# A fused linear-attention and two-layer MoE kernel: whole-tile output stores, two copying engines and two store queues in the last block, and an earlier last input product

## The chip, the cores and the metric

The kernel runs on one core of one Trainium2 chip, as one launch. The core has a matrix engine (PE, with a separate row PEld for its weight loads), a vector engine (DVE), a scalar engine (ACT), a general engine (POOL) and a sequencer that issues most DMAs (SP); ACT's sequencer can issue DMAs too. The metric is the device time of one execution in microseconds (us). Three runs of the kernel before took 1208.06, 1213.6 and 1229.15 us; the median is 1213.6 us. The profile is of one further execution.

## The reference

The inputs are six arrays of shape 4 x 8 x 768 x 40 (batch, heads, steps, head size) and five weight matrices. A recurrence over 768 steps with a 40 x 40 state for each of the 32 heads gives 3072 rows of 320 numbers. Two feed-forward layers follow, all in fp32.

```python
for t in range(S):
    y[:, :, t] = np.einsum('bhd,bhde->bhe', rt, state)
    Sa = np.einsum('bhde,bhe->bhd', state, at)
    state_decay = state * wt[:, :, None, :] - np.einsum('bhd,bhe->bhde', Sa, bt)
    state = state_decay + np.einsum('bhd,bhe->bhde', vt, kt)
x = y.transpose(0, 2, 1, 3).reshape(B * S, H * D)       # 3072 x 320
h = np.maximum(x @ w_in, 0.0); x = h * h @ w_out         # first layer, 2048 wide
g = x @ w_gate; silu = g / (1.0 + np.exp(-g))
out = silu * (x @ w_val) @ w_out2                        # second layer, 1536 wide
```

## The kernel before

The recurrence is done in chunks of 32 steps, and the first layer runs beside it, block by block. The second layer starts when the recurrence is over, and it is the last third of the program. It works on six blocks (`NB2`) of 512 rows each, as four tiles of 128 rows; of each tile, 64 rows come from one batch and 64 rows from another, because the recurrence handles two batches at a time. For each block it goes through 12 slices (`nf`) of 128 columns of the inner width, so there are 72 pairs `P` of block and slice, and the last pair is 71.

One pair (`pair2`) does this. Eight matmuls make the gate product in the PSUM bank `pg` and eight make the value product in `pv` (tag F2, line 460; every fp32 product is split in a high and a low part, hence three matmuls for one product, and a packed third for the rest of the 320 columns). ACT takes the sigmoid of `pg` (line 1461), DVE multiplies it by `pg` and then by `pv` (line 1464, twice), ACT rounds the result to its high part `gh` (line 436), and DVE makes the low part `gl` (line 1130). Then twelve matmuls, three for each of the four tiles, add the slice to four accumulators in PSUM (tag O, line 1472). After the last slice of a block ACT copies each accumulator to an SBUF tile `o2` (line 436), and SP stores it to the output (line 1481): since the 128 rows of a tile belong at two places of the output, as two DMAs of 64 rows. The view of the output is

```python
outv = out.rearrange("(r t m p) d -> m t r p d", r=nb // 2, t=2, p=64)
```

so that `outv[m, t]` has the shape 2 x 64 x 320, with the two halves 1536 rows apart.

The order on each engine is made by a planner written in the kernel (`Plan`). Each step is told to it by `op(cost, fn, reads, writes, due=..., tag=...)`: `cost` gives the engines that may run it, with a time in us that only the planner uses; a step with two engines is given to the one that would end it first. An engine takes, of the steps that are ready, the one with the smallest `due`. For pair `P` the input products have the due time `NS + DELAY + P` and the output products that plus 0.5. A DMA issue is a step of the engine whose queue it uses. `queues` maps SP and ACT to their DMA queues.

After the last pair comes a test of whether the fast recurrence stayed in range. DVE reduces the recorded maxima to `ok` (lines 1598 to 1604), PE adds them up (`cnt`, line 1606), DVE writes `flag` (line 1607), and every engine loads it and branches over a slow version of the whole computation (lines 1608 and 1609). SP then waits for every DMA that is still out before the program ends (lines 1609 and 1673).

Two other kinds of transfer matter further down. Line 1125 stores the first layer's result, 128 rows of 1280 bytes that stand one behind the other. Line 1382 (`w2_tile`) loads the second layer's weights into the tiles `ws`: for each group, first the gate matrix and then the value matrix, three loads each. The first two loads take 128 rows. The third takes the last 64 rows twice, by a source view of 2 x 64 rows into a tile of 128 partitions:

```python
return w[r0:r0 + 64, c][None].to_broadcast([2, 64, c.stop - c.start]) if last else w[r0:r0 + 128, c]
```

Of the kernel before, what the change touches and what calls it, by code (L numbers as in the profile page):

```python
# [21 lines left out]
DM = H * D  # L22
F1 = 2048
F2 = 1536
# [14 lines left out]
PE, ACT, DVE, POOL, SP = "PE", "ACT", "DVE", "POOL", "SP"  # L39
# [32 lines left out]
class Plan:  # L72
# [31 lines left out]
    def op(self, cost, fn, r=(), w=(), due=0.0, dma=0.0, take=None, give=None, cols=0, tag="", mode=None, act=0, port=False, lag=0.0):  # L104
        o = Op()
        o.cost, o.fn, o.due, o.seq, o.take, o.give, o.cols, o.tag = cost, fn, due, self.n, take, give, cols, tag
        self.n += 1
        o.dma, o.claim, o.mode, o.act, o.port, o.lag = dma, None, mode, act or cols, port, lag
        o.leaves = mode
        o.bulk = bool(cost) and SP in cost and not r  # L110
        o.succ, o.done, o.eng, o.mate = [], None, None, None
        o.ready = {e: 0.0 for e in (cost or self.free)}
        pre = set()
        for k in r:
            if k in self.writer:
                pre.add(self.writer[k])
        for k in w:
            if k in self.writer:
                pre.add(self.writer[k])
            pre.update(self.readers.get(k, ()))  # L120
        o.need = 0
        for p in pre:
            if p.done is None:
                p.succ.append(o)
                o.need += 1
            else:
                self.arrive(o, p)
        for k in r:
            self.readers.setdefault(k, []).append(o)
        for k in w:  # L130
            self.writer[k] = o
            self.readers[k] = []
        if o.need == 0:
            self.offer(o)
        return o
# [237 lines left out]
def tile_kernel(ctx: ExitStack, tc: tile.TileContext, a: dict, out: bass.AP, nb: int, seq: int):  # L373
    nc = tc.nc
# [60 lines left out]
    def copy(e, dst, src):  # L435
        nc.scalar.copy(dst, src) if e == ACT else eng[e].tensor_copy(dst, src)  # L436
# [15 lines left out]
    def in_products(ps, f, xh, xl, hi, lo, hl):  # L452
        c = slice(f * 128, (f + 1) * 128)
        seq_ = (
            (hi[0], xh[:, 0]), (hi[0], xl[:, 0]), (lo[0], xh[:, 0]),
            (hi[1], xh[:, 1]), (hi[1], xl[:, 1]), (lo[1], xh[:, 1]),
            (hl, xh[:, 2]), (hl, xl[:, 2]),
        )
        for i, (w, x) in enumerate(seq_):
            nc.tensor.matmul(ps, w[:, c], x, start=(i == 0), stop=(i == len(seq_) - 1))  # L460
# [154 lines left out]
    op = plan.op  # L615
# [101 lines left out]
    queues = {SP: nc.sync, ACT: nc.scalar}  # L717
# [410 lines left out]
    def split_pair(n, due):  # L1128
        op({ACT: t_act(512)}, lambda e: copy(e, gh[n], two["gr"][n]), (("gr", n),), (("gh", n),), due=due, tag="gh")
        op({POOL: t_pool(512), DVE: t_dve(512)}, lambda e: eng[e].tensor_sub(gl[n], two["gr"][n], gh[n].bitcast(F32)),  # L1130
           (("gr", n), ("gh", n)), (("gl", n),), due=due, tag="gl", port=True)
# [218 lines left out]
    two = {}  # L1350
# [42 lines left out]
    for g in range(NP2):  # L1393
        f = slice(g * 256, (g + 1) * 256)
        due = NS + g
# [11 lines left out]
    outv = out.rearrange("(r t m p) d -> m t r p d", r=nb // 2, t=2, p=64)  # L1407

    NB2 = NBLK // 2
    nf = F2 // 128  # L1410
    assert NBLK % 2 == 0
    acc_keys = [("p", 0), ("p", 1), ("acc", 0), ("acc", 1)]
    ACC2 = [PS[:, 4 + t] for t in range(4)]
# [29 lines left out]
    def pair2(P):  # L1443
        B, f = divmod(P, nf)
        n, b = P % NGR, P % 2
        due = NS + DELAY + P
        ks = [(x, B % 2, t) for x in ("xh2", "xl2") for t in range(4)] + ["WO"] + wkeys[("wi", 2, f // 2)]

        def f_in(kind):
            w = two["w"]  # L1450
            in_products(two["p" + kind][b], f, two["xh"][B % 2], two["xl"][B % 2],
                        *((w.hg, w.lg, w.hlg) if kind == "g" else (w.hv, w.lv, w.hlv)))

        for kind in "gv":
            op({PE: 1.814}, lambda e, kind=kind: f_in(kind), ks, (("p" + kind, b),), due=due, cols=4096, tag="F2")
        kw = dict(due=due)

        def both(x):
            return x[n].rearrange("p h t -> p (h t)")

        op({ACT: 0.478}, lambda e: nc.scalar.activation(both(two["gr"]), two["pg"][b], AF.Sigmoid), (("pg", b),), (("gr", n),),  # L1461
           tag="sig", **kw)
        for q in ("pg", "pv"):
            op({DVE: 0.602}, lambda e, q=q: nc.vector.tensor_mul(both(two["gr"]), two[q][b], both(two["gr"])), ((q, b),),  # L1464
               (("gr", n),), tag="u" + q, **kw)
        split_pair(n, due)
        wk = wkeys[("wo", 2, f // 2)]
        for t in range(4):
            def o_mm(e, t=t):
                c, w = slice(t % 2 * 128, t % 2 * 128 + 128), two["w"]  # L1470
                for i, (x, y) in enumerate(((gh, w.oh), (gh, w.ol), (gl, w.oh))):
                    nc.tensor.matmul(ACC2[t][:, :DM], x[n][:, t // 2, c], y[:, f, :], start=(f == 0 and i == 0),  # L1472
                                     stop=(f == nf - 1 and i == 2))

            op({PE: 0.44}, o_mm, [("gh", n), ("gl", n)] + wk, (acc_keys[t],), due=due + 0.5, cols=960, tag="O")
            if f == nf - 1:
                op({ACT: 0.318}, lambda e, t=t: copy(e, two["o"][t], ACC2[t][:, :DM]), (acc_keys[t],), (("o2", t),),
                   due=due, tag="o")
                d = outv[2 * B + t // 2, t % 2]
                for r in range(2):  # L1480
                    op({SP: 0.42}, lambda e, t=t, d=d, r=r: nc.sync.dma_start(d[r], two["o"][t][64 * r:64 * r + 64]),
                       (("o2", t),), (), due=due, dma=0.455, tag="dma")

    x2_load(0, NS + DELAY)
    for t in range(4):
# [1 line left out]
    for P in range(NB2 * nf):  # L1487
        B, f = divmod(P, nf)
        if B == 0:
            w2_tile(w2_d[W2[2]][f * 128:(f + 1) * 128, :], wkeys[("w2d", W2[2])] + ["WO"], DM,  # L1490
                    lambda f=f: (two["w"].oh[:, f, :], two["w"].ol[:, f, :]), ("wo", 2, f // 2), NS + DELAY + f)
        pair2(P)
        if B + 1 < NB2:
            if f == 2:
                x2_load(B + 1, NS + DELAY + P)
            if nf - 6 <= f < nf - 2:
                x2_turn(B + 1, f - (nf - 6), "pv", P % 2, NS + DELAY + P + 0.6)
# [188 lines left out]
```

## Time and profile before

| what | value |
|---|---|
| median of three runs | 1213.6 us (1208.06 to 1229.15) |
| the profiled execution | 1212.33 us |
| span of the profile, from its first to its last instruction | 1210.3 us |
| mean granted PE clock | 0.968 |
| PE busy | 1113.8 us, 92% of the span |
| DVE, ACT busy | 639.5 us (53%), 551.8 us (46%) |

The profiled execution is 2 us longer than its span. All times in the rows below are counted from the start of the span, so the program ends at 1210.3. A "q" behind an engine's name means its sequencer, which waits, branches and issues DMAs. In the table of stretches the columns are the length, the busy time of each engine, the granted PE clock (1.00 is full speed), the share of the 16 DMA engines' time that was busy, and GB/s.

### The profile page before, as it was taken

What the parts mean: (1) busy time and instruction counts of PE and PEld (TensorE: products, weight loads), DVE (VectorE), ACT (ScalarE), POOL (GpSimd) and SP (SyncE); (2) the same over time, 40 slices, a digit from 0 to 9 for tenths busy, and PEclk for the clock granted to TensorE, in tenths of its full rate; (3) what the DMA queues carried; (4) which work ended last, traced back from release to release, by engine and by line L of the source; (5) the groups of instructions that cost most, each with busy time, mean ns of one, the idle gap of its engine ahead of it and who ended that gap; (6) DMA issues with size and microseconds to landing.
All of it is one profiled execution on the core that took longest, in us unless ns stands there. A gap on an engine that the chain in (4) does not pass through costs nothing.

```text
span 1210.3 us, 42859 instructions
## 1 busy us (share of the span) xinstructions
PE 1113.8 (92%) x18640; PEld 1011.7 (84%) x18640; DVE 639.5 (53%) x1496; ACT 551.8 (46%) x1275; POOL 97.1 (8%) x122
## 2 busy tenths in 40 slices
PE   7487978989889899999998999899999999999995
PEld 7376877888888798999898899888888888888884
DVE  4766885676657475856473422445334343434432
ACT  6344985555555464645453444654223222222221
POOL 0221331011011011210000000000000000000000
PEclk9788998999999999999999999899999999999998
DMA  5645664565655465544443322422101010100001
GB/s 137 159 112 155 163 172 121 141 179 142 172 134 148 136 175 157 151 130 99 109 102 77 69 58 65 132 86 83 35 7 26 18 27 22 27 23 1 22 1 25
DMA packets 171393, 114.96 MB, mean 95 GB/s; under 512 B 104092, under 2 KB 147644, under 8 KB 171196
## 3 DMA queue, kind: packets, MB, share of 16 engines
q1 hardware_dynamic: 168556, 110.52, 35.1%
q8 instruction: 148, 2.42, 0.9%
q10 hardware_dynamic: 2640, 1.61, 0.5%
q14 instruction: 49, 0.40, 0.1%
HBM read 88.35 MB, written 23.72 MB: 93 GB/s over the span
## 4 chain that ended last, share of the span: by engine, by line
PE 67%; DMA 5%; DVE 5%; issue 3%; SPq 2%; ACT 1%; DVEq 0%; ACTq 0%
PE ps L460 31%; PE ps L465 11%; PE ps L1472 10%; DMA ws<-f_moe_w_val 3%; SPq L723 2%; PE ps L1057 2%; PE ps L1038 2%; PE ps L1029 1%; PE ps L960 1%; PE ps L973 1%; PE ps L1072 1%; PE ps L802 1%; PE ps L999 1%; PE ps L868 1%; PE ps L954 1%
## 5 line engine op out<-in xcount | busy, mean ns | idle before, releaser
L1464 DVE TENSOR_TENSOR gr<-ps,gr 128x512 f32<-128x512 f32 x144 | 99.5, 692 | 168.4 <-PE ps L460 86.4
L1146 ACT ACTIVATE ps<-ps 128x512 f32<-128x512 f32 x192 | 111.6, 581 | 106.9 <-PE ps L460 104.3
L465 PE MATMUL ps<-o1h,gh 128*128 128x320 f32 x384 | 131.9, 343 | 4.0 <-ACT gh L436 3.9
L436 ACT CAST gh<-gr 128x512 fp32r<-128x512 f32 x72 | 44.8, 622 | 177.1 <-DVE gr L1464 177.1
L465 PE MATMUL ps<-o1l,gh 128*128 128x320 f32 x384 | 121.5, 316 | 2.7 <-issue 2.7
L465 PE MATMUL ps<-o1h,gl 128*128 128x320 f32 x384 | 122.5, 319 | 0.3 <-DVE gl L413 0.3
L460 PE MATMUL ps<-xh,w1h 128*128 128x256 f32 x384 | 117.1, 305 | 0.0
L460 PE MATMUL ps<-xl,w1h 128*128 128x256 f32 x384 | 109.9, 286 | 0.0
L460 PE MATMUL ps<-xh,w1l 128*128 128x256 f32 x384 | 109.8, 286 | 0.0
L413 DVE TENSOR_TENSOR gl<-ps,gh 128x512 fp32r<-128x512 f32 x96 | 65.8, 685 | 59.0 <-ACT gh L436 58.9
L1472 PE MATMUL ps<-o2h,gh 128*128 128x320 f32 x288 | 89.0, 309 | 1.9 <-ACT gh L436 1.4
L1472 PE MATMUL ps<-o2l,gh 128*128 128x320 f32 x288 | 88.8, 308 | 0.2 <-DVE o2l L1389 0.2
L1472 PE MATMUL ps<-o2h,gl 128*128 128x320 f32 x288 | 88.7, 308 | 0.2 <-DVE gl L1130 0.2
L465 PEld LDWEIGHTS ps<-o1h,gh 128*128 128x128 f32 x384 | 74.2, 193 | 9.8 <-ACT gh L436 4.7
L1461 ACT ACTIVATE gr<-ps 128x512 f32<-128x512 f32 x72 | 43.2, 599 | 81.2 <-PE ps L460 79.6
L465 PEld LDWEIGHTS ps<-o1h,gl 128*128 128x128 f32 x384 | 74.7, 195 | 4.6 <-issue 2.5
L460 PEld LDWEIGHTS ps<-xh,w1h 128*128 128x128 f32 x384 | 74.2, 193 | 1.9
L465 PEld LDWEIGHTS ps<-o1l,gh 128*128 128x128 f32 x384 | 74.8, 195 | 0.1
L1130 DVE TENSOR_TENSOR gl<-gr,gh 128x512 fp32r<-128x512 f32 x72 | 49.9, 693 | 47.1 <-ACT gh L436 47.0
L460 PEld LDWEIGHTS ps<-xl,w1h 128*128 128x128 f32 x384 | 74.5, 194 | 0.0
L460 PEld LDWEIGHTS ps<-xh,w1l 128*128 128x128 f32 x384 | 74.1, 193 | 0.0
L1282 PE MATMUL ps<-warm 128*128 128x256 f32 x302 | 50.6, 320 | 24.3 <-DVE ct L1213 14.5
(170 smaller groups left out, 2702.8 us busy)
## 6 DMA issues: line engine op xcount, KB each, us to landing
wakb<-in_wakb_dram SPq DMA_DIRECT2D x42, 422.5 KB
RB<-in_vr_e_dram SPq DMA_DIRECT2D x44, 208.0 KB
RH<-in_r_e_dram SPq DMA_DIRECT2D x90, 80.0 KB
cx<-in_moe_w_out_dram SPq DMA_DIRECT2D x21, 320.0 KB
room<-xt_d SPq DMA_DIRECT2D x36, 128.0 KB
cx<-in_moe_w_in_dram SPq DMA_DIRECT2D x15, 256.0 KB
xt_d<-yb SPq DMA_DIRECT2D x24, 160.0 KB
x_d<-room SPq DMA_DIRECT2D x24, 160.0 KB
```

Source lines behind the costliest of these rows:

```text
L413: nc.vector.tensor_sub(dst, full, hi.bitcast(F32))
L436: nc.scalar.copy(dst, src) if e == ACT else eng[e].tensor_copy(dst, src)
L460: nc.tensor.matmul(ps, w[:, c], x, start=(i == 0), stop=(i == len(seq_) - 1))
L465: nc.tensor.matmul(acc[t][:, :DM], g[:, half, ts], w[:, f, :], start=(f == 0 and i == 0), stop=(f == nf - 1 and i == 2),)
L723: o = att(cost, lambda e: queues[e].dma_start(dst(), src()), r, w, due=due, dma=dma, tag="dma")
L1038: nc.tensor.matmul(v[64 * p:64 * p + 64, jh, u], RW[:, 4 * jh + 2 * u + p], RB[:, :, s], start=True, stop=True)
L1130: op({POOL: t_pool(512), DVE: t_dve(512)}, lambda e: eng[e].tensor_sub(gl[n], two["gr"][n], gh[n].bitcast(F32)), (("gr", n), ("gh", n)), ( ...
L1146: op({ACT: 0.478}, lambda e, f=f: nc.scalar.activation(P1[b], P1[b], f), (), (("p", b),), due=due, tag="relu")
L1282: nc.tensor.matmul(PS[:, b, 0:256].rearrange("p (a b) -> p a b", a=2), warm, warm[:, None, :].to_broadcast([128, 2, 128]), start=True, sto ...
L1461: op({ACT: 0.478}, lambda e: nc.scalar.activation(both(two["gr"]), two["pg"][b], AF.Sigmoid), (("pg", b),), (("gr", n),), tag="sig", **kw)
L1464: op({DVE: 0.602}, lambda e, q=q: nc.vector.tensor_mul(both(two["gr"]), two[q][b], both(two["gr"])), ((q, b),), (("gr", n),), tag="u" + q, ...
L1472: nc.tensor.matmul(ACC2[t][:, :DM], x[n][:, t // 2, c], y[:, f, :], start=(f == 0 and i == 0), stop=(f == nf - 1 and i == 2))
```

## The change

Four things are changed, all in the second layer.

- Every output tile is stored by one DMA of 2 x 64 rows in place of two DMAs of 64 rows.
- In the last block (`end`) the tiles 0 and 2 are copied by ACT and the tiles 1 and 3 by DVE.
- In the last block a store may be issued by SP or by ACT, as the planner finds it.
- The input products of pair 71 get a due time that is 0.6 smaller, which is before the output products of pair 70.

```diff
         for kind in "gv":
-            op({PE: 1.814}, lambda e, kind=kind: f_in(kind), ks, (("p" + kind, b),), due=due, cols=4096, tag="F2")
+            op({PE: 1.814}, lambda e, kind=kind: f_in(kind), ks, (("p" + kind, b),),
+               due=due - (0.6 if P == NB2 * nf - 1 else 0.0), cols=4096, tag="F2")
...
             if f == nf - 1:
-                op({ACT: 0.318}, lambda e, t=t: copy(e, two["o"][t], ACC2[t][:, :DM]), (acc_keys[t],), (("o2", t),),
-                   due=due, tag="o")
-                d = outv[2 * B + t // 2, t % 2]
-                for r in range(2):
-                    op({SP: 0.42}, lambda e, t=t, d=d, r=r: nc.sync.dma_start(d[r], two["o"][t][64 * r:64 * r + 64]),
-                       (("o2", t),), (), due=due, dma=0.455, tag="dma")
+                end = B == NB2 - 1
+                op(({ACT: 0.43}, {DVE: 0.45})[t % 2] if end else {ACT: 0.318}, lambda e, t=t: copy(e, two["o"][t], ACC2[t][:, :DM]),
+                   (acc_keys[t],), (("o2", t),), due=due, tag="o")
+                op({SP: 0.6, ACT: 0.6} if end else {SP: 0.6},
+                   lambda e, t=t, d=outv[2 * B + t // 2, t % 2]: queues[e].dma_start(d, two["o"][t]),
+                   (("o2", t),), (), due=due, dma=0.6, tag="dma")
```

Ahead of the last 24 output products the rest of the program has the same instructions in the same order on PE, DVE, ACT and POOL; on SP each earlier block has four stores where it had eight, at the same place between the other DMAs.

On PE, at the start of pair 71's value products; `wghl` ends the gate product of pair 71, `wvh` and `wvl` belong to its value product, and `gh0`, `gl0` are the operands of pair 70's output products. Before:

```order
L460 MATMUL ps_113<-xh21_13030,wghl_13037 128x512
L460 MATMUL ps_113<-xl21_13032,wghl_13037 128x512
L1472 MATMUL ps_113<-o2h_13427,gh0_107 128x320
L1472 MATMUL ps_113<-o2l_13428,gh0_107 128x320
L1472 MATMUL ps_113<-o2h_13427,gl0_109 128x320
L1472 MATMUL ps_113<-o2h_13427,gh0_107 128x320
```

The same place after the change:

```order
L460 MATMUL ps_113<-xh21_13030,wghl_13037 128x512
L460 MATMUL ps_113<-xl21_13032,wghl_13037 128x512
L460 MATMUL ps_113<-xh21_13030,wvh0_13038 128x512
L460 MATMUL ps_113<-xl21_13032,wvh0_13038 128x512
L460 MATMUL ps_113<-xh21_13030,wvl0_13040 128x512
L460 MATMUL ps_113<-xh21_13030,wvh1_13039 128x512
```

The eight value matmuls of pair 71 moved ahead of the twelve output matmuls of pair 70; the twelve of pair 71 still come last.

On SP, the last stores, with what each waits for (a DMAHW semaphore is that of an earlier DMA). Before:

```order
L1481 DMA out_dram<-o_13429 64x320 [waits DMAHW2_49,Activation_49]
L1481 DMA out_dram<-o_13429 64x320 [waits DMAHW3_49]
L1481 DMA out_dram<-o_13430 64x320 [waits DMAHW4_49,Activation_49]
L1481 DMA out_dram<-o_13430 64x320 [waits DMAHW5_49]
L1481 DMA out_dram<-o_13431 64x320 [waits DMAHW6_49,Activation_49]
L1481 DMA out_dram<-o_13431 64x320 [waits DMAHW7_49]
L1481 DMA out_dram<-o_13432 64x320 [waits DMAHW0_49,Activation_49]
L1481 DMA out_dram<-o_13432 64x320 [waits DMAHW1_49]
```

After the change, the last two stores of the block before, the three that SP still has in the last block, and the load of the flag behind them:

```order
L1482 DMA out_dram<-o_13431 2x64x320 [waits DMAHW4_49,Activation_49]
L1482 DMA out_dram<-o_13432 2x64x320 [waits DMAHW5_49,Activation_49]
L1482 DMA out_dram<-o_13429 2x64x320 [waits DMAHW6_49,Activation_49]
L1482 DMA out_dram<-o_13430 2x64x320 [waits DMAHW7_49,DVE_49]
L1482 DMA out_dram<-o_13432 2x64x320 [waits DMAHW1_49,DVE_49]
L1609 TENSOR_LOAD flag [waits DVE_49]
```

Eight issues became three, each with the view 2 x 64 x 320 on the output's side.

On ACT, the end of its program after the change (before, four copies stood here and no DMA):

```order
L436 CAST gh_108<-gr_13028 128x512 [waits DVE_49]
L436 COPY o_13429<-ps 128x320 [waits DMAHW2_49,PE_49]
L436 COPY o_13431<-ps 128x320 [waits DMAHW4_49,PE_49]
L1482 DMA out_dram<-o_13431 2x64x320 [waits Activation_49]
L1609 TENSOR_LOAD flag [waits DVE_49]
L1610 COMPARE_AND_BRANCH
```

Two copies went to DVE, where they stand behind the five short instructions of the range test, and the store of tile 2 came to ACT's queue.

## Rows read from the trace of the kernel before

**Rows 1.** The page's first lines: the span, then busy time by engine.

```profile
span 1210.3 us, 42859 instructions
PE 1113.8 (92%) x18640; PEld 1011.7 (84%) x18640; DVE 639.5 (53%) x1496; ACT 551.8 (46%) x1275; POOL 97.1 (8%) x122
```

**Rows 2.** The chain that ended last, its end: start us, us, what.

```profile
1193.60 1.87 PE ps L460 x8
...
1195.49 0.70 DVE gr L1464
...
1196.87 0.70 DVE gl L1130
...
1197.61 1.75 PE ps L1472 x10
...
1199.38 0.44 ACT o L436
```

**Rows 3.** Instructions in order of time, the last 20 us: start us, us, engine, line.

```profile
1191.68 0.31 PE L1472 MATMUL ps<-o2h,gh 128*128 128x320 f32 x1
1192.58 0.69 DVE L1464 TENSOR_TENSOR gr<-ps,gr 128x512 f32<-128x512 f32 x1 [2.23 <-ACT gr L1461]
1193.44 0.39 PE L460 MATMUL ps<-xh,wvh 128*128 128x512 f32 x1
1198.07 1.74 ACT L436 COPY o<-ps 128x320 f32<-128x320 f32 x4 [1.23 <-PE ps L1472]
1198.52 6.09 SPq L1481 DMA_DIRECT2D out_dram<-o  x8
```

**Rows 4.** Lines 1609 and 1673: instructions, ns min/median/max, first and last start us.

```profile
L1609 PEldq COMPARE_BRANCH  x1: 4095/4095/4095, 1200.9 to 1200.9; - x1
L1609 SPq COMPARE_BRANCH  x1: 50/50/50, 1205.8 to 1205.8; - x1
L1609 SPq EVENT_SEMAPHORE  x8: 17/17/17, 1208.3 to 1208.9; - x8
L1673 SPq EVENT_SEMAPHORE  x10: 17/28/28, 1208.9 to 1210.2; - x10
```

**Rows 5.** Stretches with stores in flight: length, engines' busy, PEclk, DMA share, GB/s.

```profile
673.50:674.00 0.50, 0.50 (x60) 0.50 (x64) 0.43 (x2) 0.49 (x1) 0.00 (x0) 1.00 0.97 341
1003.00:1004.00 1.00, 1.00 (x6) 0.83 (x5) 0.23 (x1) 0.49 (x2) 0.00 (x0) 1.00 0.51 123
1206.00:1207.00 1.00, 0.00 (x0) 0.00 (x0) 0.00 (x0) 0.00 (x0) 0.00 (x0) 0.50 0.03 8
```

**Rows 6.** SP's DMA issues in order of time, in two stretches.

```profile
672.58 0.84 SPq L1125 DMA_DIRECT2D x_d<-room  x2
...
771.02 0.50 SPq L1382 DMA_DIRECT2D ws<-f_moe_w_gate  x1
771.61 1.49 SPq L1382 DMA_DIRECT2D ws<-f_moe_w_val  x3
```

**Rows 7.** The chain that ended last, three of its pieces from 761 us on.

```profile
761.92 1.89 DMA x<-x_d
...
763.88 5.25 DMA ws<-f_moe_w_val
...
772.60 7.62 DMA ws<-f_moe_w_val
```

**Rows 8.** Two stretches behind the issues of 771 to 773 us.

```profile
774.50:775.50 1.00, 1.00 (x10) 1.00 (x9) 0.00 (x0) 0.00 (x0) 0.00 (x0) 1.00 0.15 51
775.50:776.50 1.00, 1.00 (x11) 1.00 (x10) 0.00 (x0) 0.00 (x0) 0.00 (x0) 1.00 0.13 45
```

**Rows 9.** Groups by line: a DVE copy, and store issues (ns min/median/max).

```profile
L436 DVE COPY UQ<-ps 128x320 f32<-128x320 f32 x4 | 2.0, 488 | 2.0 <-PE ps L960 1.0 <-ACT ps L436 1.0
L1481 SPq DMA_DIRECT2D out_dram<-o x48: 466/594/1688, 869.1 to 1204.0; - x48
L1125 SPq DMA_DIRECT2D x_d<-room x24: 332/367/767, 192.6 to 805.2; - x24
```

## The prediction

> **What bounds the kernel now.** I read the page first: PE is busy for 1113.8 of 1210.3 us [rows 1], so over the whole program only less PE work would pay, and the change takes none away. What it can move is the program's end, so I read the chain that ended last from its end backwards, then the last 20 us in order of time, then the sequencers' rows, and last the stretches of DMA traffic.
>
> The reader is to see three things at the end. First, PE stands still between its last input product and its last output products: the value product ends at 1195.47 (1193.60 + 1.87), a DVE product, the ACT cast and a DVE difference follow one after the other, and the output matmuls that need the low part start at 1197.61 [rows 2]. Pair 70's twelve output matmuls, which could have filled that hole, are already over: they ran from 1191.68 to 1193.44 [rows 3]. Second, PE ends at 1199.36 and the last copy at 1199.82 [rows 2], but SP issues eight stores from 1198.52 on and needs 6.09 us for them [rows 3], until 1204.61. It loads the flag and branches only then, at 1205.8, and gets to its first wait for a DMA at 1208.3; eight such waits and the closing ones take the rest, 2.0 us, to 1210.3 [rows 4]. Third, DMA traffic is as good as over in 1206 to 1207 (share 0.03) [rows 5], so those waits cost nothing: SP comes late, and the data have landed before it asks. **The end is set by SP's issues, with 5.7 us behind them (1210.3 - 1204.61).**
>
> **The change, part by part.**
>
> *The earlier input product.* Twelve matmuls of pair 70 (1193.44 - 1191.68 = 1.76 us [rows 3]) move behind pair 71's value product. That product ends 1.76 us earlier; DVE's second multiply can start at 1193.73, since the first ends at 1193.27 (1192.58 + 0.69) [rows 3]; cast and difference follow, and the low part is there at 1195.85. PE meanwhile does the twelve, until 1195.44, and the two matmuls that need only the high part, until about 1195.7, so 0.1 us of the hole is left. PE's end moves from 1199.36 to 1197.60. Gain: 1.76 us on this path.
>
> *Two engines copy.* ACT's four copies take 1.74 us back to back [rows 3], 0.435 each, and PE finishes an accumulator every 0.44 us (1.75 / 4 [rows 2]): one engine keeps pace. A DVE copy of this size from PSUM takes 0.488 [rows 9]. The last copy is now DVE's, from about 1197.62 to 1198.11; before, it ended at 1199.82. Two engines gain nothing beyond the 1.76 and lose some 0.05. The five range-test instructions that stand ahead of the DVE copies run in the wait for PE and cost nothing; without that cover they would cost under 1 us.
>
> *Fewer issues, two queues.* SP has three issues in place of eight. A 64-row store took 0.594 us to issue (median), a 128-row one 0.367 [rows 9]; the 2 x 64 load took 0.50 [rows 6]. I take 0.50. The first copy ends at about 1196.75 (1198.07 - 1.76 + 0.435), so the first issue starts at 1196.8, the third follows the last copy at 1198.15, and SP is free at 1198.65, 5.96 us earlier than 1204.61. ACT's one issue starts about 1197.65 and is over before the flag is written. If SP's issues were still what sets the end, the program would end at 1204.3.
>
> *The shape of the stores.* This is the term on which the sign hangs. The new store has 2 x 64 rows on the DRAM side and 128 partitions on the SBUF side. No store of the trace has that shape, but the third load of each weight trio has it, mirrored. Two of these were issued close together, the gate's at 771.02 and the value's at 772.60 (the third of the trio from 771.61), and the latter landed at 780.2 (772.60 + 7.62) [rows 6, 7]; the other loads of the trio are 128-row ones. From 774.5 on the DMA share is 0.13 to 0.15 at 45 to 51 GB/s [rows 8], and 45 GB/s is what carries the two loads' 262,144 bytes from 774.5 to 780.2 (5.8 us). **A share of 0.14 is two engines of sixteen (2/16 = 0.125), and two such transfers together don't reach more: they share the same two.** The value load, queued behind the gate load, took 7.62 us, one with less in its way 5.25, a plain 128-row transfer 1.89 [rows 7]. Two contiguous 128-row stores, issued from 672.58 on [rows 6], ran at 341 GB/s with a share of 0.97 [rows 5], which is 22 GB/s for each engine, so two engines would give 44 GB/s for stores as well.
>
> I take 45 GB/s. One tile is 128 x 1280 = 163,840 bytes and takes 3.64 us; the four take 14.6 us. They are issued within 2 us of each other, so they queue. The fixed part of such a transfer, start and landing, is 5.25 less 131,072 bytes at 45 GB/s (2.9), or 2.3 us. The last store lands at 1196.8 + 2.3 + 14.6 = 1213.7. SP has branched long before (1198.65 plus the 3.7 us that it took from 1204.61 to 1208.3 is 1202.4) and waits. Behind that wait are 1.4 to 2.0 us of the closing, depending on which of the eight semaphores is the late one [rows 4]; I take 1.7. **The program ends at 1215.4, 5.1 us later than now.** The 6 us that PE and SP gain are swallowed by the wait for the landing.
>
> Here the Trainium skill speaks against the change: DMA: Bandwidth & Descriptors, Why a DMA increments its semaphore by 16 and not by 1, says that a DMA runs on the largest number of engines, up to 16, that divides the outermost size of both sides. By that rule a 2 x 64 store gets 2 engines and the old 64-row store 16; the trace's loads agree (share 0.14), and no run here shows it for a store. The sum by the rule is the one above.
>
> *The earlier blocks.* Five blocks store the same way in mid-program. There 14.6 us of queued stores meet nothing: a tile of `o2` is needed again a block later, and PE has no wait on a store. The first and the last output store are 869.1 and 1204.0 [rows 9], five blocks apart, so a block lasts about 67 us. I cost it at nothing; if the cover failed, each would show up as an idle PE at a block's start.
>
> **The bounds.** Slowest: if the two engines move stores only as fast as they went in the 64-row stores, 123 GB/s at a share of 0.51 [rows 5], that is 15 GB/s each, the four take 21.7 us, and the end is at 1222.5, 12.2 us later. Fastest, with two engines for each: if ACT's store ran on other engines than SP's, three would queue (10.9 us) and the end be at 1211.7, 1.4 us later. The rate of loads of the same shape and that of contiguous stores agree, so I stay with 45 GB/s.
>
> **The rivals.**
>
> *The stores spread over all sixteen engines* (the other side, faster). For it: the contiguous 128-row store did, at 0.97 [rows 5], and the landing would be hidden as now. Against it: the loads of this very shape don't. Then SP's issues set the end at 1204.3, or 1205.9 if SP's branch takes the 4.1 us that PE's took in place of its own 2.5, because all engines now branch at once [rows 4]. That is 4.4 to 6.0 us less; about 1207.
>
> The Trainium skill has a rule that leads there: DMA: Bandwidth & Descriptors, Rules for kernel authors, advises one 128-partition transfer over two for the disjoint halves. It would make the first part a plain saving of issue time; the trace's 128-row stores fit it, the 2 x 64 loads don't.
>
> *The stores go slower still.* The 12.2 us above: two engines, at the 15 GB/s of the stores before. For it speaks that those stores are of the same tiles to the same output. Against it: they ran all sixteen engines on 64 partitions, which two engines on 128 do not. Its time is 1225.
>
> *The landing is hidden anyway.* It decides from the point at which the last store lands before SP is ready, 1202.4. With the start at 1199.1 (1196.8 + 2.3) that would need 655,360 bytes in 3.3 us, 199 GB/s, over four times what two engines showed, so it is the first rival or nothing.
>
> **How the numbers follow.** The profiled execution took 1212.33 us, 2 us more than its span, and 1.3 less than the median of 1213.6; 5.1 more makes 1217.4 from the one and 1218.7 from the other. I say 1218. Chances: two engines at about 45 GB/s for all four stores 0.66; ACT's store elsewhere 0.08 (1214 to 1215); the slow rate 0.12 (1225); all sixteen engines 0.14 (1207). The range takes in the second and third cases and most of the spread of runs, and leaves out the fourth but for its upper edge: 1208 to 1228. Every case lies within 1.1% of now, and a measurement of this kernel can tell about 2% from no change, so within 2% has 0.95; the 0.02 and 0.03 on the sides are for the spread of the runs, of which one before was 1.3% over the median.
>
> **What would show it.** Right: after 1200 a long stretch with a DMA share near 0.13 and about 45 GB/s; SP's waits at line 1610 ending near 1214 with PE, DVE and ACT idle for over 14 us; the same thin traffic for some 15 us behind each earlier block; PE without its hole before the last output products and ending near 1197.6. Wrong: a share of 0.5 and more behind the last copies and an end near 1205 (all engines), or thin traffic at about 30 GB/s and an end past 1220. The prediction falls if stores choose their engines otherwise than loads do.

## The result and the profile after

| | median us | runs | range |
|---|---|---|---|
| before, in this comparison | 1217.45 | 20 | 1207.3 to 1229.15 |
| after | 1222.62 | 20 | 1213.27 to 1236.0 |

The ratio is 1.0056, with a 95% interval of 1.0032 to 1.008: the changed kernel is slower, by 4 to 10 us, and within 2%. The ratio is of the runs in the usual state, without a few in a slower one; the medians of all runs differ by 5.2 us. Its profiled execution took 1221.75 us with a span of 1219.8 us (before 1212.33 and 1210.3 [rows 1]).

The spans differ by 9.5 us, but not all of that is the change's. The last block but one gives an anchor, the issue of its first store. First the order of time on SP in the profile after, three of the five earlier blocks and the last block:

```profile
873.39 6.03 SPq L1482 DMA_DIRECT2D out_dram<-o  x4
939.83 6.17 SPq L1482 DMA_DIRECT2D out_dram<-o  x4
...
1139.15 6.00 SPq L1482 DMA_DIRECT2D out_dram<-o  x4
...
1200.99 3.19 SPq L1482 DMA_DIRECT2D out_dram<-o  x3
```

The same stores of the kernel before:

```profile
869.13 5.03 SPq L1481 DMA_DIRECT2D out_dram<-o  x8
935.58 6.05 SPq L1481 DMA_DIRECT2D out_dram<-o  x8
...
1134.89 4.94 SPq L1481 DMA_DIRECT2D out_dram<-o  x8
```

The blocks are 66.44 us apart in both (939.83 - 873.39; before 935.58 - 869.13 = 66.45). The changed profile is 4.26 us late already at its first store, ahead of which both programs do the same, and keeps just that. So 4.26 us belong to the run. **From the anchor to the end, which I call the tail, it is 1210.3 - 1134.89 = 75.41 us before and 1219.8 - 1139.15 = 80.65 us after: the change costs 5.2 us.** The prediction had 5.1. The tail is the measure of all experiments below, because runs of one kernel differ by 20 us, and the tail leaves that out. Each kernel has one profile, so one tail; kernels that end alike agree within 0.2 us (before and e9_earlier, and e4_contig and e10_all, which ran on two chips, in the table below).

What the tail consists of shows in the chain that ended last (start, us, what), which answers to [rows 2]:

```profile
1194.25 3.69 PE ps L460 x16
...
1197.96 0.70 DVE gr L1465
...
1199.34 0.70 DVE gl L1130
...
1200.08 1.75 PE ps L1473 x10
...
1201.85 0.50 DVE o L436
```

The sixteen input matmuls now stand together, and PE goes on to 1201.83 with almost no hole. Less 4.26, that is 1197.57, 1.79 us earlier than the 1199.36 of before. PE, DVE and ACT did what the change wants. Then the end of the sequencers' work, line 1610 (the branch and the waits behind it) and line 1674 (ns min/median/max, first and last start), which answers to [rows 4]:

```profile
L1610 PEldq COMPARE_BRANCH  x1: 3455/3455/3455, 1204.6 to 1204.6; - x1
L1610 SPq COMPARE_BRANCH  x1: 50/50/50, 1207.0 to 1207.0; - x1
L1610 SPq EVENT_SEMAPHORE  x8: 17/17/17, 1214.4 to 1218.4; - x8
L1674 SPq EVENT_SEMAPHORE  x10: 17/28/28, 1218.4 to 1219.7; - x10
```

Before, the eight waits came within 0.6 us [rows 4]; now the first is passed at 1214.4 and the last at 1218.4. SP stands there and waits for DMAs. The stretches show which (columns as in [rows 5]):

```profile
1204.00:1205.00 1.00, 0.00 (x0) 0.00 (x0) 0.00 (x0) 0.00 (x0) 0.00 (x0) 1.00 0.13 31
1212.00:1213.00 1.00, 0.00 (x0) 0.00 (x0) 0.00 (x0) 0.00 (x0) 0.00 (x0) 0.50 0.14 52
1217.00:1218.00 1.00, 0.00 (x0) 0.00 (x0) 0.00 (x0) 0.00 (x0) 0.00 (x0) 0.50 0.04 14
1218.00:1219.00 1.00, 0.00 (x0) 0.00 (x0) 0.00 (x0) 0.00 (x0) 0.00 (x0) 0.50 0.00 0
```

No engine computes, and for 15 us two of sixteen DMA engines (0.125) carry the output, first at some 30 and then at some 50 GB/s. The traffic stops just before SP's last wait is passed. By queue (packets, MB, share), from 1207 to 1213:

```profile
q1 hardware_dynamic: 105, 0.13, 6.5%
q10 hardware_dynamic: 104, 0.13, 6.1%
q14 instruction: 5, 0.04, 2.0%
```

q1 is SP's queue and q10 ACT's: with SP alone (e7_sponly) q10 moves nothing behind the last copies. The two together have 12.6%, so SP's and ACT's stores run on the same two engines. Instructions are loaded beside them (q14) and add to the share, which reaches 0.27 in one of the 15 us (1205 to 1206) and 0.15 to 0.18 in four (1207 to 1211).

The trace also records when each increment of a DMA's semaphore came, though not its size. A store of 64 rows gives sixteen; a store of 2 x 64 rows gives three, one just behind its issue and two as it lands. The last store landed at 1217.92, 16.93 us behind the first issue.

### The profile page after: what moved, and what is told of

Read it like the earlier page. It is cut to its first block, busy times and chain, and to the rows that moved or that the text cites. A ratio compares the mean times of both kernels' runs of the same rounds, so it can differ in the third digit from the quotient of the medians.

```text
span 1219.8 us, 42834 instructions
## 1 busy us (share of the span) xinstructions
PE 1122.4 (92%) x18640; PEld 1020.4 (84%) x18640; DVE 641.2 (53%) x1498; ACT 550.8 (45%) x1273; POOL 97.1 (8%) x122
## 4 chain that ended last, share of the span: by engine, by line
PE 68%; DMA 8%; SPq 3%; issue 2%; DVE 2%; ACT 1%; DVEq 0%; ACTq 0%
PE ps L460 31%; PE ps L465 11%; PE ps L1473 10%; SPq L723 3%; DMA ws<-f_moe_w_val 3%; PE ps L1057 2%; PE ps L1038 2%; PE ps L1029 2%; DMA RB<-in_vr_e_dram 2%; PE ps L960 1%; PE ps L1072 1%; PE ps L973 1%; PE ps L802 1%; PE ps L999 1%; PE ps L868 1%
## 5 line engine op out<-in xcount | busy, mean ns | idle before, releaser
L1282 PE MATMUL ps<-warm 128*128 128x256 f32 x302 | 54.8, 340 | 25.8 <-DVE ct L1213 13.6
```

Of the source, the lines that this page charges most:

```text
L1282: nc.tensor.matmul(PS[:, b, 0:256].rearrange("p (a b) -> p a b", a=2), warm, warm[:, None, :].to_broadcast([128, 2, 128]), start=True, sto ...
```

## The experiments

The theory: a store whose view of the output has two places of 64 rows runs on two DMA engines, and the landing of four of these sets the end. Its rivals: ACT's queue or the copies on DVE cost the time; one transfer of 164 KB takes long whatever its shape; the distance between the places is what costs; the earlier blocks' stores cost it.

| kernel | what differs | tail expected | tail measured |
|---|---|---|---|
| before | | | 75.41 |
| after | | | 80.65 |
| e1_early | before + early input product | 73.65 | 1202.6 - 1128.85 = 73.75 |
| e2_shape | before + 2 x 64 stores in the last block, SP alone | 82.4 | 1215.1 - 1133.24 = 81.86 |
| e3_split | after, all stores as two of 64 rows | 70.0 to 71.7 | 1204.9 - 1133.69 = 71.21 |
| e4_contig | after, last block's tiles in one piece each | 69.3 to 71.0 | 1199.9 - 1129.25 = 70.65 |
| e6_four | after, last block's tiles in four pieces each | 73.4 | 1207.7 - 1132.72 = 74.98 |
| e7_sponly | after, SP alone issues | 80.65 | 1218.3 - 1137.88 = 80.42 |
| e8_act | after, ACT alone copies | 80.65 | 1213.4 - 1132.90 = 80.50 |
| e9_earlier | before + 2 x 64 stores in the earlier blocks | 75.4 | 1212.9 - 1137.36 = 75.54 |
| e10_all | as e4_contig, in all blocks | 70.65 | 1236.3 - 1165.47 = 70.83 |

### e1_early: the early input product alone

```diff
-            op({PE: 1.814}, lambda e, kind=kind: f_in(kind), ks, (("p" + kind, b),), due=due, cols=4096, tag="F2")
+            op({PE: 1.814}, lambda e, kind=kind: f_in(kind), ks, (("p" + kind, b),),
+               due=due - (0.6 if P == NB2 * nf - 1 else 0.0), cols=4096, tag="F2")
```

> The kernel before with the early input product alone: stores, copies and queues as before. Measure for all runs: the tail, from the issue of the first store of the last block but one to the end of the span (before 1210.3 - 1134.89 = 75.41 us, changed kernel 1219.8 - 1139.15 = 80.65 us). Theory (the shape of the stores sets the loss, the early product gains what PE no longer idles): PE's hole closes, SP still issues eight stores behind the copies, tail 73.65 us (1.76 less than before). Rival (the moved product gains nothing, because the copies or SP set the end anyway): 75.4. Rival (the moved product is itself the loss): about 80.

The tail is 73.75 us, 1.66 less than before. The early product is worth what was claimed, and the end follows PE, because SP's eight issues follow the copies. One run took 1204.63 us beside a median of 1212.11 for the kernel before (23 runs, 1201.64 to 1221.73), which tells nothing by itself.

### e2_shape: the shape of the last block's stores alone

```diff
+                if B == NB2 - 1:
+                    op({SP: 0.6}, lambda e, t=t, d=d: nc.sync.dma_start(d, two["o"][t]), (("o2", t),), (), due=due, dma=0.6, tag="dma")
-                for r in range(2):
+                for r in range(2) if B < NB2 - 1 else ():
```

> The kernel before with one part of the change alone: in the last block each tile is stored by one transfer of two places of 64 rows, SP issuing all four; copies by ACT, the order of products and the earlier blocks as before. Theory (a store to two places runs on two DMA engines, 3.64 us a tile, and the landing of the fourth sets the end): first issue as before, last landing about 17 us behind it, tail 82.4 us (7.0 more than before). Rival (the loss comes from two queues or from two engines copying): the tail stays at 75.4 or falls with the fewer issues to about 73. Rival (the loss comes from the earlier blocks' stores): 75.4 too.

The store issues in order of time, and two of the stretches behind them:

```profile
1133.24 4.94 SPq L1483 DMA_DIRECT2D out_dram<-o  x8
...
1196.87 6.57 SPq L1481 DMA_DIRECT2D out_dram<-o  x4
```

```profile
1199.00:1200.00 1.00, 0.00 (x0) 0.00 (x0) 0.00 (x0) 0.00 (x0) 0.00 (x0) 1.00 0.13 31
1211.00:1212.00 1.00, 0.00 (x0) 0.00 (x0) 0.00 (x0) 0.00 (x0) 0.00 (x0) 0.50 0.13 49
```

The first store comes 63.63 us behind the anchor, as before (1198.52 - 1134.89), so nothing ahead of it moved. With SP alone and ACT's copies, the shape by itself costs 6.45 us. The landing of the last came 16.7 us behind the first issue. And a row of its own: **four issues took SP 6.57 us, where eight of 64 rows took 6.09 [rows 3].** Fewer issues did not free SP.

### e3_split: two queues, two copying engines, stores of 64 rows

```diff
-                op({SP: 0.6, ACT: 0.6} if end else {SP: 0.6},
-                   lambda e, t=t, d=outv[2 * B + t // 2, t % 2]: queues[e].dma_start(d, two["o"][t]),
-                   (("o2", t),), (), due=due, dma=0.6, tag="dma")
+                for r in range(2):
+                    op({SP: 0.6, ACT: 0.6} if end else {SP: 0.6},
+                       lambda e, t=t, r=r, d=outv[2 * B + t // 2, t % 2]: queues[e].dma_start(d[r], two["o"][t][64 * r:64 * r + 64]),
+                       (("o2", t),), (), due=due, dma=0.3, tag="dma")
```

> The changed kernel with every tile stored as two transfers of 64 rows again, in all blocks; in the last block both queues issue them (four each), two engines copy, and the input product is early. Theory: all sixteen DMA engines carry each transfer, the last landing comes about 2.3 us behind the last issue, and the tail is 70.0 to 71.7 us (3.7 to 5.4 less than before, 9 to 10.6 less than the changed kernel), about 1213 us where the kernel before takes 1217. Rival (ACT's queue or the copies on DVE cost the time): the tail stays near 80.6. Rival (issues never set the end, the closing does): 73.6, as with the early product alone.

```profile
1133.69 4.94 SPq L1483 DMA_DIRECT2D out_dram<-o  x8
...
1195.53 2.50 SPq L1483 DMA_DIRECT2D out_dram<-o  x4
1195.53 1.39 ACTq L1483 DMA_DIRECT2D out_dram<-o  x2
1197.07 1.26 ACTq L1483 DMA_DIRECT2D out_dram<-o  x2
```

The tail is 71.21 us: 9.4 less than after and 4.2 less than before. With the early product alone it was 73.75, so the two queues help once the stores run on all engines: the last issue ends 64.64 us behind the anchor here and 67.73 in e1_early. The second copying engine doesn't help: the last copy ends at 63.78 here, at 63.12 with ACT alone in e1_early. By the clock the gain isn't shown: 1207.95 us median of 12 runs, ratio to before 0.9998 (0.9962 to 1.0034), an interval that just holds the 4.2 / 1212 = 0.35% that the tail gives.

### e4_contig: the same size of store, in one piece

The rows of the last block are dealt to its tiles anew, so that a tile is 128 rows in a row of the output; the loads of these four tiles take two places of 64 rows each.

```diff
+    outw = out.rearrange("(r t n) d -> r t n d", r=nb // 2, t=2)
...
+            end = B == NB2 - 1
+            src = x2v[2 * B:2 * B + 2, t % 2, 64 * (t // 2):64 * (t // 2) + 64] if end else x2v[2 * B + t // 2, t % 2]
...
+        d = outw[t // 2, t % 2, 128 * B:128 * B + 128]
```

> The changed kernel with the rows of the last block dealt to its four tiles in another way: each tile holds 128 rows that lie in one piece in the output (and is loaded from two places instead). Four stores of 128 rows on two queues as in the changed kernel, the same bytes, the same engines. Theory (two places are the cost, not 128 rows in one transfer): the stores run on all sixteen DMA engines, tail 69.3 to 71.0 us. Rival (a transfer of 164 KB takes that long whatever its shape): tail 80.6. Rival (the loads of two places at the block's head now come late): the distance from the anchor to the first store of the last block grows beyond the changed kernel's 61.84 us.

Its stores in order of time, two stretches, and lines 1617 and 1681 (the branch and the last waits):

```profile
1129.25 5.96 SPq L1489 DMA_DIRECT2D out_dram<-o  x4
...
1191.09 1.72 SPq L1489 DMA_DIRECT2D out_dram<-o  x3
...
1191.97 0.39 ACTq L1489 DMA_DIRECT2D out_dram<-o  x1
```

```profile
1192.00:1193.00 1.00, 0.19 (x2) 0.11 (x2) 0.59 (x2) 0.00 (x0) 0.00 (x0) 1.00 0.95 333
1193.00:1194.00 1.00, 0.00 (x0) 0.00 (x0) 0.00 (x0) 0.00 (x0) 0.00 (x0) 1.00 0.85 304
```

```profile
L1617 SPq EVENT_SEMAPHORE  x8: 17/17/17, 1198.0 to 1198.5; - x8
L1617 PEldq COMPARE_BRANCH  x1: 3635/3635/3635, 1193.9 to 1193.9; - x1
L1617 SPq COMPARE_BRANCH  x1: 50/50/50, 1194.2 to 1194.2; - x1
L1681 SPq EVENT_SEMAPHORE  x10: 17/28/28, 1198.6 to 1199.8; - x10
```

The same bytes in as many transfers on the same queues, and a DMA share of 0.95 at 333 GB/s in place of 0.14 at 50. That excludes the size of a transfer, ACT's queue and the DVE copies as causes. The first store comes 61.84 us behind the anchor, as after (1200.99 - 1139.15), so the loads of two places at this block's head cost nothing. The last store landed 3.2 us behind the first issue, at 1194.3. SP had branched at 1194.2, and its first wait is passed only at 1198.0: now it is the branch, some 3.8 us for SP and 3.6 for PE, that sets the end.

By the clock it is 1206.1 us (median of 12) beside 1212.11, ratio 0.996 (0.9928 to 0.9992): **this version is faster than the kernel before**, by as much as its tail says (4.76 / 1212 = 0.39%), which is less than 2%. It was not timed beside the changed kernel; there only the tails speak, 70.65 against 80.65.

### e6_four: four places

```diff
+    outf = out.rearrange("(r m p) d -> m r p d", r=nb, p=64)
...
-                   lambda e, t=t, d=outv[2 * B + t // 2, t % 2]: queues[e].dma_start(d, two["o"][t]),
+                   lambda e, t=t, d=outf[2 * B + t // 2, :, 32 * (t % 2):32 * (t % 2) + 32] if end else outv[2 * B + t // 2, t % 2]: queues[e].dma_start(d, two["o"][t]),
```

> The changed kernel with the last block's rows dealt so that each tile's store goes to four places of 32 rows (and its load comes from four places in two transfers). Theory (as many DMA engines as places): four engines, about twice the rate of the two, the four tiles take about 7.3 us instead of 14.6, tail about 73.4 us. Rival (distant places are the cost, more of them cost more): 80.6 or above. Rival (anything but one piece falls to two engines): 80.6.

```profile
1198.00:1199.00 1.00, 0.00 (x0) 0.00 (x0) 0.00 (x0) 0.00 (x0) 0.00 (x0) 0.54 0.26 97
1200.00:1201.00 1.00, 0.00 (x0) 0.00 (x0) 0.00 (x0) 0.00 (x0) 0.00 (x0) 0.50 0.25 73
1203.00:1204.00 1.00, 0.00 (x0) 0.00 (x0) 0.00 (x0) 0.00 (x0) 0.00 (x0) 0.50 0.25 43
1204.00:1205.00 1.00, 0.00 (x0) 0.00 (x0) 0.00 (x0) 0.00 (x0) 0.00 (x0) 0.50 0.18 35
```

The share is 0.25, four of sixteen, and the semaphore of each store gets five increments (one and four). Four places at half the distance are faster than two, so more places don't cost by themselves. More engines land the stores sooner, but not in proportion: two 16.9 us behind the first issue, four 11.25, sixteen 3.2 (e4_contig). The distance alone was not varied for a store. Against it as the cause speaks that the third weight load of before takes the same 64 rows twice, at no distance, and also ran at a share of 0.13 to 0.15 [rows 8]. The tail of 74.98 us is 1.6 above what twice the rate would give. The last store landed 11.25 us behind the first issue in place of 9.6, since the rate fell to 73 and then 43 GB/s at the same share (in 1203 to 1204 the loading of instructions has 0.05 of it). Why these four engines went slower there was not settled.

The Trainium skill states the pattern (DMA: Bandwidth & Descriptors, Why a DMA increments its semaphore by 16 and not by 1): for DMAs that SP and ACT issue, the issuing sequencer writes those of the 16 increments whose engines take no part at once, and each engine that does adds one when its data has landed. The counts here agree for stores: sixteen for 64 rows and for 128 rows in one piece, one and two for two places, one and four for four.

### e7_sponly and e8_act: one queue, one copying engine

```diff
-                op({SP: 0.6, ACT: 0.6} if end else {SP: 0.6},
+                op({SP: 0.6},
```

> The changed kernel with SP alone issuing the last block's stores. Theory (the two DMA engines are busy from the first store to the last landing, whoever issues): the first store starts as before, tail 80.65 us, within 0.4. Rival (ACT's queue costs the time, its packets alternating with SP's): tail about 75 to 77. Rival (ACT's issue helps): SP's fourth issue behind three others, tail above 81.5.

```diff
-                op(({ACT: 0.43}, {DVE: 0.45})[t % 2] if end else {ACT: 0.318}, lambda e, t=t: copy(e, two["o"][t], ACC2[t][:, :DM]),
+                op({ACT: 0.43} if end else {ACT: 0.318}, lambda e, t=t: copy(e, two["o"][t], ACC2[t][:, :DM]),
```

> The changed kernel with ACT alone copying the last block's four tiles (two queues, early input product and stores of two places as in the changed kernel). Theory (the first tile's copy comes at the same time, the landings hide the rest): tail 80.65 us, within 0.4. Rival (the copies on DVE, behind its range test, cost the time): tail 2 us or more less than 80.65.

The last block's issues with SP alone:

```profile
1199.72 6.68 SPq L1482 DMA_DIRECT2D out_dram<-o  x4
```

The tails are 80.42 and 80.50 us, 0.23 and 0.15 below the changed kernel: with the stores on two DMA engines neither the second queue nor the second copying engine matters. The copies themselves come no sooner with two engines either: the last ends 63.13 us behind the anchor with ACT alone and 63.19 with both. With SP alone the stores land one after the other (5.9, 9.7, 13.5 and 16.7 us behind the first issue); with both queues the second and the third land late together (13.7 and 13.4), and the last at 16.9. The order changes and the end does not.

### e9_earlier: the earlier blocks alone

```diff
+                if B < NB2 - 1:
+                    op({SP: 0.6}, lambda e, t=t, d=d: nc.sync.dma_start(d, two["o"][t]), (("o2", t),), (), due=due, dma=0.6, tag="dma")
-                for r in range(2):
+                for r in range(2) if B == NB2 - 1 else ():
```

> The kernel before with the change's stores in the earlier blocks alone: one transfer of two places per tile in all blocks but the last, the last block as before (eight transfers of 64 rows, ACT copies, no early product). Theory (the earlier blocks' landings are hidden): blocks still 66.44 us apart by their first stores, tail 75.4 us, within 0.3. Rival (their slow landings, or SP's longer issues, hold back later loads or the last block's first store): blocks further apart than 66.44, or a tail above 76.

The tail is 75.54 us, and the blocks' first stores are 66.44 us apart (938.04 - 871.60). The earlier blocks' stores cost nothing.

### e10_all: one piece in every block

```diff
-            src = x2v[2 * B + t // 2, t % 2]
+            src = x2v[2 * B:2 * B + 2, t % 2, 64 * (t // 2):64 * (t // 2) + 64]
```

> The changed kernel with every block's rows dealt as in the kernel whose last block stored 128 rows in one piece, so that all stores go to one piece and all loads come from two. Theory (earlier blocks cost nothing either way): tail as there, 70.65 us, within 0.3; time 0.3 to 0.5% under the kernel before, as its tail is 4.76 us shorter (0.39% of 1212). Rival (loads of two places now hold up the start of each block): blocks further apart than 66.44 us and no gain against the kernel before.

The tail came as expected, 70.83 us, and the time did not: 1240.51 us beside 1219.27, ratio 1.0199 (1.016 to 1.0237). Here my expectation was wrong, and neither was the rival quite right, because the blocks stay 66.44 us apart (966.15 - 899.71). What is late is the layer's start. SP's issues there, first of the kernel before, then of this one (`x` are the layer's input tiles, `ws` its weights):

```profile
755.39 2.26 SPq L1419 DMA_DIRECT2D x<-x_d  x4
...
761.42 1.89 SPq L1419 DMA_DIRECT2D x<-x_d  x4
...
765.47 5.46 SPq L1419 DMA_DIRECT2D x<-x_d  x8
771.02 0.50 SPq L1382 DMA_DIRECT2D ws<-f_moe_w_gate  x1
```

```profile
756.69 9.67 SPq L1425 DMA_DIRECT2D x<-x_d  x4
...
768.08 8.20 SPq L1425 DMA_DIRECT2D x<-x_d  x4
...
781.50 17.14 SPq L1425 DMA_DIRECT2D x<-x_d  x8
798.73 1.52 SPq L1382 DMA_DIRECT2D ws<-f_moe_w_gate  x1
...
899.71 2.16 SPq L1488 DMA_DIRECT2D out_dram<-o  x4
```

The last eight loads, of two places, took SP 17.14 us to issue, in place of 5.46, and all sixteen 35.01 in place of 9.61, which is 25.4 more. A single issue took up to 3.25 us, where before it was at most 0.93. I read this as an issue lasting longer while the two engines still have earlier transfers queued, as the fourth store of each earlier block did too (up to 3.55 us). The weights stand behind the loads on SP's queue, and PE waits for the weights, as the chain that ended last shows:

```profile
844.06 6.76 DMA ws<-f_moe_w_val
...
852.28 5.40 PE ps L1479 x35
```

The same products start at 821.68 in the kernel before, also behind a weight load. The first store of the layer comes at 899.71, where e9_earlier on the same chip had it at 871.60: 28.1 us later, less the 4.7 us that the tail wins, makes 23.4; the medians differ by 21.2, and the ratio says 24.3.

## Why the prediction was right

**The early input product.** Predicted 1.76 us, measured 1.66 (e1_early) with nothing else changed.

**Two engines copying.** Predicted to gain nothing: with ACT alone (e8_act) the last copy ends 0.06 us sooner behind the anchor, and the tails agree within 0.15 us. The last copy of the changed kernel ended at 1202.35, less 4.26 is 1198.09, where 1198.11 was predicted.

**Fewer issues.** This term was mis-sized, without harm to the sum. Predicted were 0.50 us an issue and SP free at 1198.65. The first two took 0.51 each, the third 1.81, and SP was free at 1204.18, less 4.26 is 1199.92. An issue behind queued two-engine transfers is long, which no row of before showed; the wait for the landing covered it here, and nothing covered it in e10_all.

**The shape of the stores.** The term that carries the sign. Predicted were two engines, 45 GB/s, the last landing 16.9 us behind the first issue; measured were a share near 0.13 and 16.93 us. That the time fits to 0.1 us is luck in part. The first 3 us ran at 26 to 31 GB/s, which is the bound of 15 GB/s an engine for a moment. From the first landing (1207.22) to the last the other three tiles took 10.70 us, 46 GB/s, with instructions loaded beside them; in mid-program the same stores land 3.3 us apart, 49 GB/s. And one support of the 45 doesn't hold: the two weight loads' 262,144 bytes did not all move between 774.5 and 780.2, since the gate load had been under way before and landed at 776.53. The rates of the stretches [rows 8] and the 22 GB/s for each engine [rows 5] do. Two contiguous halves (e3_split) and one piece (e4_contig) took the loss away, the shape alone brought it (e2_shape), and four places gave something between (e6_four). Predicted closing behind the landing 1.7 us, measured 1219.8 - 1217.92 = 1.88. Less 4.26 the program ended at 1215.5, where 1215.4 was predicted.

**The parts add up.** 75.41 - 1.66 (e1_early) + 6.45 (e2_shape) = 80.20, and the whole change has 80.65. The 0.45 that are left are the two queues, the copies and the spread of single profiles; e7_sponly and e8_act leave 0.23 and 0.15 to the first two.

**The earlier blocks.** Predicted at nothing, measured at nothing (e9_earlier, and 66.44 us between blocks).

**ACT's store on other engines** fell: SP's and ACT's stores shared the same two. Their queues had 6.5% and 6.1% together, SP's alone has 12.7% in the same stretch of e7_sponly (1206 to 1212), and the end is the same.

**The first rival** was right in what it would be worth. Had all sixteen engines carried the stores, it said 4.4 to 6.0 us less than before, the smaller gain if the branch takes as long for SP as for PE. e4_contig has 4.76 less, and SP's branch took 3.8 us in place of the 2.5 of before [rows 4].

**The absolute number.** 1218 was the earlier median plus 5.1. In the comparison the kernel before had a median of 1217.45, not 1213.6, and the ratio times 1217.45 adds 6.8 (3.9 to 9.7), which holds the tail's 5.2. The measured median, 1222.62, is 4.6 above 1218, and 3.85 of that is the other base.

## What to carry to other kernels

Count a transfer's engines before its issues: on both sides the outermost dimension of the view should be many rows, not two places, for here two engines landed 16.9 us behind the first issue what sixteen landed in 3.2. Such transfers were free as long as nothing waited for their landing and nothing urgent stood behind them on their queue; at the program's end the first failed, and ahead of loads that an engine waits for the second did. Where runs differ by more than the effect, measure from an anchor in the trace behind which the two programs begin to differ.

## What the runs showed of the hardware that was not expected

The sequencer's time to issue a DMA is not a constant: on SP a 2 x 64 store took 0.512 us with little queued and up to 3.552 with three of its kind ahead (group of line 1482 in the profile after), a 2 x 64 load 17.14 / 8 = 2.1 us on average:

```profile
L1482 SPq DMA_DIRECT2D out_dram<-o x23: 512/578/3552, 873.4 to 1202.4; - x23
```

In each of the 30 earlier blocks stored this way (after, e4_contig, e6_four, e7_sponly, e8_act, e9_earlier) the fourth issue ended 0.2 to 0.4 us behind the landing of the block's first store, as if SP had stood in it until then; why is not shown. A transfer of 2 x 64 rows also holds up others: in the kernel before, a 128-row weight load issued at 771.61, behind the gate's 2 x 64 load, had fourteen of its increments by 774.59 and the last two only at 776.88.

Two engines carried only 22 to 32 GB/s in the first 3 us of a burst (1202 to 1205 and, in mid-program, 1140 to 1143 of the profile after), and about 50 afterwards. When the stores no longer set the end, the branch behind the range test does: from the branch to SP's first wait it is 3.8 us in e4_contig, with no data in its way. That wasn't tried further.
